# A decode step on one core: paired group semaphores, and the projection and second FFN product computed the other way round

## The chip, the cores and the metric

The kernel runs on one core of a Trainium2 chip. The metric is the device time of one execution in microseconds, taken as the median of several runs; lower is better. Beside the times there is one profiled execution, from which every duration below comes. PE is the matrix engine, PEld its weight loads, DVE the vector engine, ACT the scalar engine, POOL is GpSimd, and SP is the queue that issues the DMAs.

## The reference

It is one decode token for a batch of two. The input `x` is layer-normalised; attention with 32 heads over a cache of 8192 positions and a small dense network both read the result, and both outputs are added to `x`:

```python
# x: (2, 1, 512); caches: (2, 32, 8192, 128); wq: (512, 4096); wo: (4096, 512)
# w1: (512, 1792); w2: (1792, 512); all bf16
xn = layernorm(x)
q = (xn @ wq) split into 32 heads
p = softmax(q @ k_cache.T * 128 ** -0.5)
o = p @ v_cache
y = relu(xn @ w1) @ w2
return x + o.reshape(2, 1, 4096) @ wo + y
```

The two caches are 268 MB together. The weights add 12 MB.

## The kernel before

**Pairs.** The 64 combinations of batch and head are worked off two at a time, so there are 32 pairs. A pair's K is one tile of 4 MB (`ks`, two buffers), its V another (`vs`, two buffers). In a tile, each of the 128 partitions holds 128 cache rows of 128 elements. These 128 rows are taken in 16 groups of 8 (`NG`, `EG`).

**One step on PE** (L337 to L361) does this for a pair: for each group it transposes the 8 blocks of K into PSUM (`tp`, L301), DVE or ACT copies them to SBUF (`kT`, L416), and two groups later PE forms the scores with the query (`Sc`, L308). Which engine copies a group is set by `ON_ACT`. Between and after these, PE multiplies the previous pair's probabilities with its V (`weighted`, L321). In the middle of that it does two small matmuls for the softmax maximum (L356, L359). The steps run in a hardware loop of 16 passes with two pairs each; each engine counts the pairs in a register, which it compares with the semaphores.

**Semaphores per group.** Group `e` has its own two: `pT[e]`, raised when its transposes are done, and `kR[e]`, raised when its copy is done. They go up by one per pair, and the wait is for the pair's number `n`. SP waits for the last group's `pT` before it loads the K after next into the same buffer (L189), and for `sW` before it loads the next V (L191).

**Order of the DMAs.** Everything large goes through SP's queue in program order: `wq` (into `vs[1]`), `w1`, `w2`, then K and V of the pairs in turn, then the last V in two halves with semaphores of their own (`dH`), then `wo` in five pieces of 14, 7, 6, 3 and 2 blocks (`cuts`), each with its own semaphore (`dWo`). All five are issued some 30 us before the end, and they land in the order in which they were issued.

**Start.** Before the loop PE forms the queries (L247) and the first FFN product (L260); then the second FFN product with the activations as the stationary operand. The 2 activation columns are padded to 32 (`CT`), so that the four quarters of the 512 outputs go to four column groups of the array: 14 x 4 matmuls of 128 moving columns (L278). Four more matmuls add the input `x` (L286). The result `y` is a tile of 128 partitions, of which eight rows hold values: a quarter and a batch entry each. DVE copies it to `ys`.

**Tail.** After the loop PE sums the softmax denominators (L376), multiplies the last probabilities with the last V (L321), and rearranges the result (L386, L391) into `OX`, again padded to 32 columns. Then it multiplies with `wo` in the same manner: `OX` is stationary, and each of the 32 blocks of `wo` gives four matmuls of 128 moving columns, one for each quarter (L405), which wait piece by piece. DVE adds `ys` (L512), and SP stores the eight rows (L166). A last wait on GpSimd and the clearing of the semaphores end the program.

Of the kernel before, what the change touches and what calls it, by code (L numbers as in the profile page):

```python
# [11 lines left out]
R = 2  # L12
EG = 8
NG = 16
REP = 32
ON_ACT = (0, 3, 5, 8, 11, 13)


@with_exitstack
def kernel(  # L20
# [39 lines left out]

    CT = P // KT
    CB = CT // Bsz
    assert KT * Bsz * CB == P
    ctx.enter_context(tc.tile_critical(no_gpsimd_drain=True))
# [18 lines left out]
    kT = [sb([P, EG, P], bf16, f"kT{i}") for i in range(4)]  # L83
    identb = sb([P, P], bf16, "identb")
    sel = sb([H, DQ, P], bf16, "sel")
    onesh = sb([P, 2, P], f32, "onesh")
# [22 lines left out]
    Ob = sb([H, Bsz, Dh], bf16, "Ob")  # L109
    OX = sb([P, WJ, CT], bf16, "OX")  # L110
    hT = sb([P, FJ, CT], bf16, "hT")
    ys = sb([P, P], f32, "ys")
    osb = sb([P, P], bf16, "osb")
    onex = sb([Bsz, CT], bf16, "onex")

# [17 lines left out]
    dV = [sem(f"dV{i}") for i in range(R)]  # L133
    dH = [sem(f"dH{i}") for i in range(2)]
    dW = [sem(f"dWo{i}") for i in range(5)]
    sG, sI, sQ, sQ1 = sem("sG"), sem("sI"), sem("sQ"), sem("sQ1")
    sV, sA, sE = sem("sV"), sem("sA"), sem("sE")
    sS, sT, sB, sW = sem("sS"), sem("sT"), sem("sB"), sem("sW")
    pT = [sem(f"pT{e}") for e in range(NG)]
    kR = [sem(f"kR{e}") for e in range(NG)]  # L140
    sM, sX, sP, sO, sN = sem("sM"), sem("sX"), sem("sP"), sem("sO"), sem("sN")
# [6 lines left out]
    cuts = (0, 14, 21, 27, 30, WJ)  # L148
    NC = len(cuts) - 1
    qp = ot[0][0:QG * Bsz, :]  # L150
    tpq = tp[1][:].rearrange("p g k -> p (g k)")[:, 0:N].rearrange(
# [5 lines left out]
    hp = ot[1][:, 0:FJ * Bsz].rearrange("p (j b) -> p j b", b=Bsz)  # L157
    y = Sc[1][:, 0:P]
    fin = ot[0][:, 0:P]

    def cols(ap, c):
        return ap[c * CT:(c + 1) * CT, :]


    def store(eng):
        eng.dma_start(  # L166
            out.rearrange("b s (c p) -> c (b s) p", p=P),
            osb[0:P - CB + 1:CB, :],
        ).then_inc(dO, 16)

# [10 lines left out]
    @(lambda f: f(nc.sync))  # L181
    def _(sp):
        sp.dma_start(w1_sb, B_w1.rearrange("(p kt) f -> p kt f", kt=KT)).then_inc(dW1, 16)  # L183
        sp.dma_start(w2_sb, B_w2.rearrange("(p j) n -> p j n", j=FJ)).then_inc(dW2, 16)  # L184
        load_k(0)
        load_k(1)
        load_v(0)
        for t in range(NP - 2):
            sp.wait_ge(pT[NG - 1], t + 1)  # L189
            load_k(t + R)  # L190
            sp.wait_ge(sW, t + 1)  # L191
            load_v(t + 1)
        sp.wait_ge(sW, NP - 1)
        for i in range(2):
            sl = slice(i * SLOT // 2, (i + 1) * SLOT // 2)
            sp.dma_start(  # L196
                vs[(NP - 1) % R][:, sl], V_all[(NP - 1) * P:NP * P, sl]
            ).then_inc(dH[i], 16)
        for c in range(NC):
            sl = slice(cuts[c], cuts[c + 1])  # L200
            sp.dma_start(wo_sb[:, sl, :], wo_v[:, sl, :]).then_inc(dW[c], 16)  # L201
        sp.wait_ge(sE, 1)
        store(sp)


    @(lambda f: f(nc.gpsimd))
    def _(g):
# [16 lines left out]
        for u in range(2):  # L224
            g.memset(onesh[u * HP:(u + 1) * HP, u, :], 1.0).then_inc(sI, 1)
            g.wait_ge(sI, 3 + u)
        g.memset(OX[:], 0.0).then_inc(sI, 1)
        g.wait_ge(sV, 100)
# [8 lines left out]
    def _(pe):  # L237
# [38 lines left out]
        for j in range(FJ):  # L276
            for c in range(KT):
                pe.matmul(  # L278
                    cols(y, c),
                    lhsT=hT[:, j, :],  # L280
                    rhs=w2_sb[:, j, c * P:(c + 1) * P],
                    start=(j == 0),
                    stop=False,
                )
        for c in range(KT):
            i = pe.matmul(  # L286
                cols(y, c),
                lhsT=onex[:],
                rhs=xsb[:, c * P:(c + 1) * P],
                start=False,  # L290
                stop=True,
            )
# [5 lines left out]
        def transposes(r, e):  # L298
            for i in range(EG):
                kk = e * EG + i  # L300
                t = pe.transpose(tp[e % 4][:, i, :], ks[r][:, kk * Dh:(kk + 1) * Dh], identb[:])  # L301
            t.then_inc(pT[e], 1)

        def scores(r, e, n):
            pe.wait_ge(kR[e], n)
            for i in range(EG):
                kk = e * EG + i
                t = pe.matmul(  # L308
                    Sc[r][:, 2 * kk:2 * kk + 2 * REP],
                    lhsT=kT[e % 4][:, i, :],  # L310
                    rhs=rep(q2[r][:]),
                    start=True,
                    stop=True,
                )
            if e == NG - 1:
                t.then_inc(sS, 1)
# [19 lines left out]

        def step(r, n, n16):  # L337

# [3 lines left out]
            for e in range(NG):  # L342
                transposes(r, e)
                if e >= 2:
                    scores(r, e - 2, n)
            v = 1 - r
            values(v, n, n16)
            weighted(v, 0)
            scores(r, NG - 2, n)
            weighted(v, 1)  # L350
            scores(r, NG - 1, n)
            for e in range(2, NG):
# [9 lines left out]

        reg = nc.alloc_register(mybir.EngineType.PE, "pairno")
        pe.reg_mov(reg, 0)
        with pe.Fori(16, 16 * (NP // R) + 1, 16) as n16:
            for r in range(R):
                pe.reg_add(reg, reg, 1)
                step(r, reg, n16)

# [5 lines left out]
        for u in range(2):  # L375
            t = pe.matmul(dbp[:, :, u], lhsT=onesh[:, u, :], rhs=RS[:], start=True, stop=True)  # L376
        t.then_inc(sH, 1)
        for i in range(2):
            pe.wait_ge(dH[i], 16)
            for e in range(i * NG // 2, (i + 1) * NG // 2):  # L380
# [20 lines left out]
        for c in range(NC):  # L401
            pe.wait_ge(dW[c], 16)
            for j in range(cuts[c], cuts[c + 1]):
                for k in range(KT):
                    t = pe.matmul(  # L405
                        cols(fin, k),
                        lhsT=OX[:, j, :],
                        rhs=wo_sb[:, j, k * P:(k + 1) * P],
                        start=(j == 0),
                        stop=(j == WJ - 1),  # L410
                    )
        t.then_inc(sH, 1)

    def kcopy(eng, e):
        fn = eng.copy if e in ON_ACT else eng.tensor_copy
        fn(kT[e % 4][:], tp[e % 4][:]).then_inc(kR[e], 1)  # L416


    @(lambda f: f(nc.vector))
    def _(v):  # L420
        v.memset(eps_t[:], eps).then_inc(sV, 1)
        v.memset(onesb[:], 1.0)
        v.memset(xz[:], 0.0).then_inc(sZ, 1)
        v.memset(onex[:], 0.0)
        v.memset(hT[:], 0.0).then_inc(sZ, 1)
        v.memset(prm[R - 1][:], 0.0).then_inc(sP, 1)
# [16 lines left out]
        v.wait_ge(sQ, 1)  # L443
        v.wait_ge(sI, 1)
        v.wait_ge(sZ, 1)
# [5 lines left out]
        ).then_inc(sV, 1)  # L451
        v.wait_ge(sZ, 2)
        v.tensor_copy(onex[:, 0:CT:CB], identb[0:Bsz, 0:Bsz])
        v.wait_ge(sF, 1)
        v.tensor_scalar(
            out=hT[:, :, 0:CT:CB], in0=hp, scalar1=0.0, scalar2=None, op0=ALU.max,
        ).then_inc(sF, 1)
# [6 lines left out]
        v.wait_ge(sF, 3)  # L464
        v.tensor_copy(ys[:], y).then_inc(sF, 1)

        def pair(i, n):
            for e in range(NG):
                if e not in ON_ACT:
                    v.wait_ge(pT[e], n)  # L470
                    kcopy(v, e)
            v.wait_ge(sS, n)
# [11 lines left out]

        reg = nc.alloc_register(mybir.EngineType.DVE, "pairno_v")
        v.reg_mov(reg, 0)
        with v.Fori(0, NP // R):
            for r in range(R):
                v.reg_add(reg, reg, 1)
                pair(r, reg)  # L490

# [14 lines left out]
        v.wait_ge(sH, 3)  # L506
        v.wait_ge(sI, 5)
        v.tensor_copy(
            OX[:, :, 0:CT:CB], Sc[1][:, 0:Bsz * WJ].rearrange("p (b j) -> p j b", b=Bsz)
        ).then_inc(sV, 1)  # L510
        v.wait_ge(sH, 4)
        v.tensor_tensor(out=osb[:], in0=fin, in1=ys[:], op=ALU.add).then_inc(sE, 1)  # L512


    @(lambda f: f(nc.scalar))
    def _(a):
# [9 lines left out]

        def pair(i, n, t):
            for e in range(NG):
                if e in ON_ACT:
                    a.wait_ge(pT[e], n)  # L530
                    kcopy(a, e)
            a.wait_ge(sB, n)
# [15 lines left out]
        a.copy(nm[0][:, 0:1], eps_t[:]).then_inc(sO, 1)  # L548
        reg = nc.alloc_register(mybir.EngineType.Activation, "pairno_a")
        a.reg_mov(reg, 0)  # L550
        with a.Fori(0, NP // R) as tr:
            for r in range(R):
                a.reg_add(reg, reg, 1)
                pair(r, reg, tr * R + r)
# [28 lines left out]
```

## Time and profile before

| | us |
|---|---|
| median of 5 runs | 662.39 (662.02 to 662.48) |
| the profiled execution's own time | 662.47 |
| its span on the core | 660.5 |
| PE busy | 555.3 |
| DVE busy | 254.1 |
| ACT busy | 255.8 |

The span is the time between the first and the last instruction that the profile keeps; 2.0 us of the execution's time lie around it. A line of the groups names the source line, the engine, the operation, what it writes and reads, and the number of such instructions, then their busy time and the mean of one. A line of a timeline has the start, the length, and in brackets how long the engine stood idle before it and what released it; "issue" there means that it waited for nothing that the profile shows. The DMA row has one digit for each fortieth of the span, the mean busy share of the 16 DMA engines in tenths. Matmuls are pipelined, so that a group's length is less than its number times the time of one.

Three groups that the change touches, and one that stands for the loop:

```profile
L301 PE MATMUL tp<-identb,ks 128*128 128x128 bf16 x4096 | 324.3, 229 | 71.4 <-DMA ks<-in_A_k_cache_dram 71.4
L278 PE MATMUL Sc<-w_sb,hT 128*32 128x128 bf16 x56 | 1.7, 312 | 0.2 <-DVE hT L455 0.2
L286 PE MATMUL Sc<-xsb,onex 2*32 2x128 bf16 x4 | 0.3, 283 | 0.0
L405 PE MATMUL ot<-w_sb,OX 128*32 128x128 bf16 x128 | 3.5, 250 | 4.5 <-DMA w_sb<-in_A_wo_dram 3.5 <-DVE OX L508 0.6 <-issue 0.3
```

### The profile page before, as it was taken

To read this page: it belongs to the slowest core of one execution; us is meant where nothing else is said; L and a number is where in the kernel's file an instruction comes from. 1 tells how busy PE (TensorE), PEld (TensorE's weight loads), DVE (VectorE), ACT (ScalarE), POOL (GpSimd) and SP (SyncE) were. 2 spreads that over 40 slices of the span, in tenths; PEclk is the share of its full clock that TensorE was granted. 3 is DMA by queue.
4 is the path that set the end of the run, shared out by engine and by line. 5 is a ranking of instruction groups with operands and counts; after the bars stand their busy time and mean duration, and the time that the engine had idled before them with its cause. 6 is when DMAs were issued, how large, how long until landed. Compare 5 with 4: busy or idle time off the path is not lost.

```text
span 660.5 us, 26934 instructions
## 1 busy us (share of the span) xinstructions
PE 555.3 (84%) x12774; PEld 533.8 (81%) x12774; DVE 254.1 (38%) x438; ACT 255.8 (39%) x403; POOL 9.5 (1%) x45
## 2 busy tenths in 40 slices
PE   1788899987989878879987887997878898887894
PEld 0487898987879878879987887987878898887893
DVE  1143344442434433334443343443434344343341
ACT  1034445442434434434353433344343443433330
POOL 2000000000000000000000000000000000000000
PEclk9799999998998988999898899898989998898997
DMA  8999999999999999999999999999999999999995
GB/s 364 431 439 427 429 433 431 437 427 433 431 433 437 427 433 429 433 439 427 433 429 433 439 427 433 429 433 437 425 437 429 433 437 425 437 429 433 437 419 237
DMA packets 10539, 280.67 MB, mean 425 GB/s; under 512 B 1182, under 2 KB 1184, under 8 KB 1696
## 3 DMA queue, kind: packets, MB, share of 16 engines
q1 hardware_dynamic: 10524, 280.50, 98.9%
q8 instruction: 9, 0.15, 0.1%
q14 instruction: 2, 0.02, 0.0%
q10 hardware_dynamic: 4, 0.00, 0.0%
HBM read 280.50 MB, written 0.00 MB: 425 GB/s over the span
## 4 chain that ended last, share of the span: by engine, by line
DMA 58%; PE 37%; ACT 2%; issue 1%; SPq 1%; ACTq 0%; DVE 0%
DMA ks<-in_A_k_cache_dram 54%; PE tp L301 21%; PE Sc L308 11%; DMA w_sb<-in_A_wo_dram 5%; PE ot L321 4%; ACT kT L416 2%; ACT L416 1%; SPq L201 0%; PE Sc L356 0%; SPq L196 0%; PE Sc L359 0%; PE ot L405 0%; SPq L184 0%; SPq L183 0%; SPq L177 0%
## 5 line engine op out<-in xcount | busy, mean ns | idle before, releaser
L301 PE MATMUL tp<-identb,ks 128*128 128x128 bf16 x4096 | 324.3, 229 | 71.4 <-DMA ks<-in_A_k_cache_dram 71.4
L416 DVE COPY kT<-tp 128x1024 bf16<-128x1024 bf16 x320 | 219.7, 691 | 329.5 <-PE tp L301 329.2
L301 PEld LDWEIGHTS tp<-identb,ks 128*128 128x128 bf16 x4096 | 255.8, 103 | 75.3 <-DMA ks<-in_A_k_cache_dram 74.7
L416 ACT COPY kT<-tp 128x1024 bf16<-128x1024 bf16 x192 | 194.3, 1012 | 235.7 <-PE tp L301 235.6
L308 PE MATMUL Sc<-q,kT 128*128 128x64 bf16 x4096 | 217.1, 196 | 8.2 <-ACT kT L416 5.5
L308 PEld LDWEIGHTS Sc<-q,kT 128*128 128x128 bf16 x4096 | 178.8, 100 | 11.3 <-ACT kT L416 8.8
L321 PE MATMUL ot<-prm,vs 128*128 128x64 bf16 x4224 | 156.1, 192 | 3.2 <-issue 3.2
L321 PEld LDWEIGHTS ot<-prm,vs 128*128 128x128 bf16 x4224 | 139.1, 97 | 6.1 <-issue 3.4
L533 ACT COPY nm<-Sc 128x2 f32<-128x2 f32 x32 | 5.1, 160 | 120.9 <-PE Sc L359 120.9
L537 ACT ACTIVATE prm<-Sc,nm 64x128 bf16<-64x128 f32 x64 | 25.8, 404 | 4.3
L475 DVE TENSOR_REDUCE mcol<-Sc 64x1 bf16<-64x128 f32 x64 | 18.6, 291 | 17.6 <-PE Sc L308 17.2
L416 ACT ACT_TABLE_LOAD x16 | 20.5, 1283 | 2.2
L247 PE MATMUL ot<-vs,xz 128*16 128x512 bf16 x32 | 9.6, 474 | 8.1 <-DMA vs<-in_A_wq_dram 8.1
L480 DVE TENSOR_REDUCE mx<-Sc 1x2 bf16<-1x128 bf16 x32 | 8.9, 278 | 16.9 <-PE Sc L356 16.9
L247 PEld LDWEIGHTS ot<-vs,xz 128*16 128x16 bf16 x32 | 3.3, 106 | 14.0 <-issue 11.7
L232 POOL COPY q<-qb 128x2 bf16<-128x2 bf16 x32 | 5.8, 184 | 588.7 <-PE Sc L308 566.1
L525 ACT COPY OTf<-ot 128x2 f32 x32 | 5.1, 160 | 22.4 <-PE ot L321 22.4
L537 ACT ACTIVATION_READ_ACCUMULATOR prm<-Sc,nm x64 | 11.8, 184 | 0.0
L449 DVE TENSOR_SCALAR qs<-ot 16x512 bf16<-16x512 f32 x1 | 0.7, 680 | 17.6 <-PE ot L247 17.6
L405 PE MATMUL ot<-w_sb,OX 128*32 128x128 bf16 x128 | 3.5, 250 | 4.5 <-DMA w_sb<-in_A_wo_dram 3.5
L356 PE MATMUL Sc<-identb,mcol 128*1 128x128 bf16 x32 | 7.0, 217 | 0.0
L405 PEld LDWEIGHTS ot<-w_sb,OX 128*32 128x32 bf16 x128 | 2.2, 106 | 5.6 <-DMA w_sb<-in_A_wo_dram 4.5
(55 smaller groups left out, 36.3 us busy)
## 6 DMA issues: line engine op xcount, KB each, us to landing
ks<-in_A_k_cache_dram SPq DMA_DIRECT2D x32, 4096.0 KB, 26.7
vs<-in_A_v_cache_dram SPq DMA_DIRECT2D x31, 4096.0 KB, 31.3
vs<-in_A_wq_dram SPq DMA_DIRECT2D x1, 4096.0 KB, 12.4
vs<-in_A_v_cache_dram SPq DMA_DIRECT2D x2, 2048.0 KB, 19.3
w_sb<-in_B_w_dram SPq DMA_DIRECT2D x2, 1792.0 KB, 18.1
w_sb<-in_A_wo_dram SPq DMA_DIRECT2D x1, 1792.0 KB, 25.3
w_sb<-in_A_wo_dram SPq DMA_DIRECT2D x1, 896.0 KB, 27.0
w_sb<-in_A_wo_dram SPq DMA_DIRECT2D x1, 768.0 KB, 28.4
```

The lines of the kernel that those rows point to most:

```text
L232: g.tensor_copy(q2[t % R][:], qb[:, 2 * t:2 * t + 2]).then_inc(sQ1, 1)
L247: i = pe.matmul(qp, lhsT=xz[:, kt, Z - g * Bsz:Z - g * Bsz + QG * Bsz], rhs=vs[1][:, (kt * QG + g) * 512:(kt * QG + g + 1) * 512], start=( ...
L301: t = pe.transpose(tp[e % 4][:, i, :], ks[r][:, kk * Dh:(kk + 1) * Dh], identb[:])
L308: t = pe.matmul(Sc[r][:, 2 * kk:2 * kk + 2 * REP], lhsT=kT[e % 4][:, i, :], rhs=rep(q2[r][:]), start=True, stop=True,)
L321: t = pe.matmul(ot[r][:, 0:2 * REP], lhsT=vs[r][:, kk * Dh:(kk + 1) * Dh], rhs=rep(prm[r][:, kk, :]), start=(kk == 0), stop=(kk == KB - 1),)
L356: pe.transpose(tr_of(r), mcol[r][:], identb[:]).then_inc(sT, 1)
L405: t = pe.matmul(cols(fin, k), lhsT=OX[:, j, :], rhs=wo_sb[:, j, k * P:(k + 1) * P], start=(j == 0), stop=(j == WJ - 1),)
L416: fn(kT[e % 4][:], tp[e % 4][:]).then_inc(kR[e], 1)
L475: m = v.tensor_reduce(out=mcol[i][half, :], in_=S_of(i)[half, :, u], axis=AX.X, op=ALU.max)
L480: v.tensor_reduce(out=mx[i][:], in_=tr_of(i).rearrange("o (u m) -> o u m", u=2), axis=AX.X, op=ALU.max, negate=True,).then_inc(sX, 1)
L525: a.copy(OTf[:, bass.ds(c, 2)], ot[r][:, 0:2]).then_inc(sO, 1)
L537: x = a.activation(out=prm[i][half, :, u], in_=S_of(i)[half, :, u], func=ACTF.Exp, bias=nm[i][half, u:u + 1], scale=1.0, accum_out=RS[half ...
```

## The change

It has three parts.

**Semaphores.** Groups `e` and `e + 8` share one `pT` and one `kR`. In pair `n` the first raises it to `2n - 1` and the second to `2n`, so that each engine keeps two more registers with these values. The two halves of the last V are counted on `dW1` and `dW2`, which the FFN weights used at the start, and the first piece of `wo` on `dX`, which the load of `x` used; these waits are for 32 in place of 16. There are 19 semaphores fewer. Which engine copies which group stays the same.

**Second FFN product.** The 2 activation columns are stationary without padding, and all 512 columns of a block of `w2` move: 14 matmuls. DVE adds `x` when it takes the result out, so that `ys` is 2 x 512 in f32.

**Projection with `wo`.** Each 128 x 128 part of `wo` is the stationary operand and the 2 columns of `OX` move; the result has the outputs along the partitions, 8 columns in all. The FFN result with `x` is put in first, by four f32 matmuls with a 2 x 2 identity, ahead of the last V's product. At the end the 8 columns are copied, transposed on PE to 8 rows, copied again, and stored.

```diff
-    pT = [sem(f"pT{e}") for e in range(NG)]
-    kR = [sem(f"kR{e}") for e in range(NG)]
+    HG = NG // 2
+    pT = [sem(f"pT{e}") for e in range(HG)]
+    kR = [sem(f"kR{e}") for e in range(HG)]
...
+    last = [(dW1, 32), (dW2, 32)]
+    piece = [(dX, 32)] + [(sem(f"dWo{c}"), 16) for c in range(1, NC)]
...
-            sp.wait_ge(pT[NG - 1], t + 1)
+            sp.wait_ge(pT[HG - 1], 2 * (t + 1))
...
-        store(sp)
+        sp.dma_start(
+            out.rearrange("b s (c p) -> (b s c) p", p=P), osb[:]
+        ).then_inc(dO, 16)
+    def advance(eng, n, h):
+        eng.reg_add(n, n, 1)
+        eng.reg_add(h[0], h[1], 1)
+        eng.reg_add(h[1], h[1], 2)
...
-        g.memset(OX[:], 0.0).then_inc(sI, 1)
+        g.memset(ident2[:], 0.0).then_inc(sG, 1)
+        g.wait_ge(sG, 5)
+        g.affine_select(
+            out=ident2[:], in_=ident2[:], compare_op=ALU.not_equal, fill=1.0,
+            base=0, pattern=[[-1, Bsz]], channel_multiplier=1,
+        ).then_inc(sI, 1)
...
         for j in range(FJ):
-            for c in range(KT):
-                pe.matmul(cols(y, c), lhsT=hT[:, j, :],
-                    rhs=w2_sb[:, j, c * P:(c + 1) * P], start=(j == 0), stop=False)
-        for c in range(KT):
-            i = pe.matmul(cols(y, c), lhsT=onex[:],
-                rhs=xsb[:, c * P:(c + 1) * P], start=False, stop=True)
+            i = pe.matmul(y, lhsT=hT[:, j, :], rhs=w2_sb[:, j, :],
+                start=(j == 0), stop=(j == FJ - 1))
...
-            t.then_inc(pT[e], 1)
+            t.then_inc(pT[e % HG], 1)
-        def scores(r, e, n):
-            pe.wait_ge(kR[e], n)
+        def scores(r, e, h):
+            pe.wait_ge(kR[e % HG], h[e // HG])
...
         t.then_inc(sH, 1)
+        for k in range(KT):
+            pe.matmul(fin[:, k, :], lhsT=ys[:, k * P:(k + 1) * P], rhs=ident2[:],
+                start=(k == 0), stop=False)
         for i in range(2):
-            pe.wait_ge(dH[i], 16)
+            pe.wait_ge(*last[i])
...
-                    t = pe.matmul(cols(fin, k), lhsT=OX[:, j, :],
-                        rhs=wo_sb[:, j, k * P:(k + 1) * P],
-                        start=(j == 0), stop=(j == WJ - 1))
+                    t = pe.matmul(fin[:, k, :], lhsT=wo_sb[:, j, k * P:(k + 1) * P],
+                        rhs=OX[:, j, :], start=False,
+                        stop=(j == WJ - 1 and k == KT - 1))
         t.then_inc(sH, 1)
+        pe.wait_ge(sV, 106)
+        pe.transpose(tp[1][0:Bsz * KT, 0, :],
+            yT[:].rearrange("p b c -> p (b c)"), identb[:]).then_inc(sH, 1)
...
-        v.tensor_copy(ys[:], y).then_inc(sF, 1)
+        v.tensor_tensor(out=ys[:], in0=y, in1=xsb[:], op=ALU.add).then_inc(sF, 1)
...
         v.wait_ge(sH, 4)
-        v.tensor_tensor(out=osb[:], in0=fin, in1=ys[:], op=ALU.add).then_inc(sE, 1)
+        v.tensor_copy(yT[:], ot[0][:, 0:KT * Bsz].rearrange("p (b c) -> p b c", c=KT)).then_inc(sV, 1)
+        v.wait_ge(sH, 5)
+        v.tensor_copy(osb[:], tp[1][0:Bsz * KT, 0, :]).then_inc(sE, 1)
```

## The prediction

> **What bounds the kernel now.** I read the page first, then what the DMA queue waited for, then the last 20 us as a timeline, then that stretch in small windows.
>
> ```profile
> span 660.5 us, 26934 instructions
> DMA  8999999999999999999999999999999999999995
> q8 instruction: 9, 0.15, 0.1%
> ks<-in_A_k_cache_dram SPq DMA_DIRECT2D x32, 4096.0 KB, 26.7
> SPq L172 <- PE tp L301: 432.1, 30, 41.6
> ```
>
> The DMA row is full in all but the first and last slice: 280.5 MB bound the time. A K load lands 26.7 us after its issue, though 4 MB take 9.8 us at 430 GB/s; so some 17 us of transfers are ahead of each K load, and whatever makes SP issue a few us later in the loop costs nothing. What can move the time is the first slice, the last one, and the end. q8 carries nine instruction packets of 16 KB; they matter below.
>
> ```profile
> 643.75 4.07 PE L321 MATMUL ot<-prm,vs 128*128 128x64 bf16 x128
> 649.61 0.83 PE L405 MATMUL ot<-w_sb,OX 128*32 128x128 bf16 x45 [0.58 <-DVE OX L508]
> 650.75 0.35 PE L405 MATMUL ot<-w_sb,OX 128*32 128x128 bf16 x11 [0.31 <-issue]
> 651.70 0.57 PE L405 MATMUL ot<-w_sb,OX 128*32 128x128 bf16 x28 [0.60 <-DMA w_sb<-in_A_wo_dram]
> 656.58 0.40 PE L405 MATMUL ot<-w_sb,OX 128*32 128x128 bf16 x8 [1.55 <-DMA w_sb<-in_A_wo_dram]
> 657.04 0.29 DVE L512 TENSOR_TENSOR osb<-ot,ys 128x128 bf16<-128x128 f32 x1 [7.56 <-PE ot L405]
> 657.36 0.71 SPq L166 DMA_DIRECT2D out_dram<-osb  x1
> ```
>
> At the end PE waits for wo's pieces; the fifth (2 of 32 blocks) lands last, then come eight matmuls, one add, the store. But that landing is odd (start and length, busy time of PE, PEld, DVE, ACT, POOL, then clock, DMA share, GB/s):
>
> ```profile
> 654.40:654.70 0.30, 0.19 (x9) 0.18 (x12) 0.00 (x0) 0.00 (x0) 0.00 (x0) 0.50 0.06 21
> 654.72:655.48 0.76, 0.31 (x12) 0.04 (x4) 0.00 (x0) 0.00 (x0) 0.00 (x0) 0.50 0.00 0
> 655.48:655.74 0.26, 0.00 (x0) 0.00 (x0) 0.00 (x0) 0.00 (x0) 0.00 (x0) 0.50 0.06 8
> ```
>
> wo is through by 654.70 but for one 2 KB row, which moves alone at 655.49. By the trace's packet records an instruction packet of 16,384 B starts at 654.396 and takes 1.11 us; the row follows at its end, so both sit on one DMA engine. By the semaphore records 15 of the fifth piece's 16 increments are in by 655.107, the last at 656.536. **The end of the kernel hangs on one instruction fetch: 1.43 us.**
>
> Where does it come from? PE stops for instructions ("issue") at times. In the loop's first pass it stops after 62 weighted matmuls of pair 0 (stall ending at 50.33), in the tail after 45 wo matmuls (650.74). Counted in the code, 636 load-matmul pairs and 9 waits, register and branch steps lie between, 1281 instructions: 5 times 256 and one. So a block is 256 instructions, and each boundary that PE passes asks for the block after the next. From a stall's end to the next packet it took 4.67 us (50.33 to 55.00), 3.63 (57.47 to 61.10), 4.75 (69.76 to 74.51) and 3.66 (650.74 to 654.40). That last packet lies beyond the program's end: useless, yet it holds wo.
>
> [...]
>
> **The change part by part.**
>
> *Shared semaphores.* Pair n raises a shared counter from 2n-2 to 2n-1 (group e) and 2n (group e+8), so every wait opens on the same event as before; SP's wait on the last group too. Two more register steps per pair on PE, DVE and ACT (32 to 42 ns each in the trace's records) hide in PE's 71.4 us of waiting for K and the engines' longer ones; without that cover they would be 32 x 2 x 0.04 = 2.6 us. At the end 72 semaphores (66 named in the code, 6 of the frame) are cleared one by one from 659.76 to 660.13, 5.2 ns each; 19 fewer: -0.10 us. The late loads' semaphores are only other counters: 0.
>
> *FFN2 at the start.* 60 column-tiled matmuls (26.90 to 28.81) become 14 of 512 columns. L247 has that shape: 9.61 us for 32, 0.30 each, at most 0.43: 4.2 to 6.0 us, so done by 31.1 to 33.0. K of pair 0 lands at 32.98 (PE idles 4.18 us before it): hidden. If it ran over, K2's issue at 45.45 would slip; the 20.4 MB queued ahead last until about 49.5, 4 us of cover. DVE's add waits in front of the first copy at 34.91: also covered. GpSimd swaps the OX memset (0.96 us) for two small operations, 20 us before its next job.
>
> *Residual as four f32 matmuls in the tail.* L376 shows two f32 matmuls as four load-matmul pairs, 0.109 us apart; four make eight: 0.87 us. 128 weighted matmuls, OX and wo queue behind: wo's start moves from 649.61 to 650.48. That is cover as long as wo's pieces land later than PE gets to them.
>
> *wo with weights stationary.* 128 full loads of 128 columns with 2 moving. The nearest rows: L321, contiguous weights, load 97 ns, 4.07 us for 128, 31 ns each; and L260, 2 moving columns but weights at a stride, load 163 ns, 3.52 us for 56, 60 ns. The wo slice is contiguous, so I take 31. Pieces one and two are done at 652.2 and 653.1, piece three lands about 653.5 and ends at 654.3, four (654.47) at 654.9: PE waits for the fifth.
>
> [...]
>
> *The code moves.* Before wo stand 46 pairs fewer (FFN2: -92 instructions), one register move, some 2 register steps and eight pairs more (+19): -73. Boundaries stay, so that after 45 wo matmuls falls after 81, and the one before it, now after weighted matmul 51 (645.3), after 88 (644.62 + 2.73 = 647.4). Its block took 5.4 us to be there (650.74): now 652.8, when PE reaches matmul 81 at 653.0; up to 0.5 us of stall would be lost in PE's waits. Past it the useless packet is asked for at 652.8 or later; with 3.6 to 4.75 us it starts after 656.4, and wo is through at 654.7. **So the fifth piece lands at about 655.11: -1.43 us.**
>
> *The tail.* From landing to store, now 656.54 to 657.36: 0.82. After: wake 0.04, eight matmuls 7 x 0.031 + 0.20 = 0.42, hop 0.03, copy of 128x8 0.165 (L446), hop 0.05, transpose 0.224 (L386), hop 0.04, copy of 8x128 0.22 (between L453's 0.149 and L505's 0.280), hop 0.03: 1.22, +0.40. Bounds: 1.05, and 1.6 at half clock with both copies at 0.28. PE waits on the first copy and DVE on the transpose, with only the store behind them. The store has 8 plain rows in place of a 4x2 pattern: its issue takes 0.71, SP's others 0.33 to 0.43, the small x load 0.55 (ACT's queue). I take the slowest of SP's own, 0.43: -0.28 (0 to -0.38).
>
> **Sum:** -1.43 + 0.40 - 0.28 - 0.10 = -1.41. The profiled run took 662.47 (span 660.5, 2.0 around it), the median 662.39: 661.06 and 660.98; I say **661.0**.
>
> **Rivals.**
> 1. *The packet still meets wo's last row.* Delays of under 2 us would do it. For: nothing fixes the delay, and queues are thinner at the end. Against: all four measured are 3.6 or more. The 1.43 is then not gained: 662.39 + 0.40 - 0.38 = 662.4.
> 2. *PE starves at matmul 81.* If the block takes 7.2 us (4.75 + 2.45 from packet to release) it arrives at 654.6; 47 matmuls are left, 1.5 us, 0.65 later than forecast: 661.7, at worst 662.3.
> 3. *Slower: the weight load at 60 ns.* Should 2 moving columns, not the stride, be what makes L260 slow, PE becomes the bound: 650.48 + 128 x 0.06 + 0.17 = 658.33; then 0.76 to the store, 659.1 against 657.36, less 0.38: +1.36, 663.75. It decides from 38 ns on and is a loss from 49. The load's own 163 against 97 ns speaks against it.
> 4. *Other groups released too early or late by the shared counts:* excluded by the order of increments, and the DMA cover would hide some us.
>
> **How the numbers follow.** Forecast 0.66 (660.5 to 661.5), first rival 0.14, second 0.10, third 0.08, the rest 0.02. The range 660.4 to 662.8 takes in the first three. 0.2% is 1.32 us, about what a measurement here tells from no change: faster means below 661.07, slower above 663.71. The forecast lies on the first edge, its sum just past it; I put two thirds of it below, as most terms could still come out cheaper: faster 0.45. Its other third and rivals one and two make the same 0.45; slower 0.10.
>
> **What would show it.** The fifth piece's matmuls begin near 655.15, with no DMA in a lone late window; the "issue" gap in wo goes from matmul 45 to about 81; eight f32 pairs of about 0.9 us before the weighted run; wo spaced by about 31 ns; from the last wo matmul to the store two copies and a transpose, 0.76 us. I am wrong if the last row still moves alone, if wo's load takes 163 ns, or if a slice of the loop loses DMA share.

## The result, and the profile after

The changed kernel takes 660.69 us in the median (660.50 to 661.47 over 25 runs); beside it the kernel before took 662.27 (660.87 to 662.57 over 45 runs). The ratio, which is taken over the means, is 0.9979, with a 95% interval of 0.9974 to 0.9985: 1.4 us less, and 1.58 between the medians. The profiled execution took 660.65 us against 662.47.

First the page of the changed kernel, with its DMA row and its instruction queue:

```profile
span 658.6 us, 26862 instructions
...
DMA  8999999999999999999999999999999999999996
...
q8 instruction: 9, 0.15, 0.1%
```

The loop runs as before: the slices between the first and the last are full as they were, and there are nine instruction packets as before. The last slice has a 6 where it had a 5. The span is 1.9 us shorter, so look at the end. The timeline of the changed kernel from 640 us on (start, length, what, idle time before it and its releaser):

```profile
642.40 1.05 PE L379 MATMUL ot<-ident,ys 2*128 2x2 f32 x8
643.38 4.08 PE L322 MATMUL ot<-prm,vs 128*128 128x64 bf16 x128
...
649.34 1.54 PE L413 MATMUL ot<-OX,w_sb 128*128 128x2 bf16 x56 [0.69 <-DMA w_sb<-in_A_wo_dram]
651.44 0.91 PE L413 MATMUL ot<-OX,w_sb 128*128 128x2 bf16 x28 [0.56 <-DMA w_sb<-in_A_wo_dram]
653.35 1.39 PE L413 MATMUL ot<-OX,w_sb 128*128 128x2 bf16 x36 [1.01 <-DMA w_sb<-in_A_wo_dram]
654.98 0.38 PE L413 MATMUL ot<-OX,w_sb 128*128 128x2 bf16 x8 [0.24 <-DMA w_sb<-in_A_wo_dram]
655.39 0.17 DVE L517 CAST yT<-ot 128x8 bf16<-128x8 f32 x1 [6.47 <-PE ot L413]
655.61 0.27 PE L422 MATMUL tp<-identb,yT 128*8 128x128 bf16 x1 [0.26 <-DVE yT L517]
655.92 0.21 DVE L519 COPY osb<-tp 8x128 bf16<-8x128 bf16 x1 [0.36 <-PE tp L422]
656.16 0.37 SPq L195 DMA_DIRECT2D out_dram<-osb  x1
```

The last eight matmuls start at 654.98, not at 656.58: PE waits 0.24 us for the fifth piece, where it waited 1.55. Behind them stand the two copies and the transpose; still the store is issued at 656.16 in place of 657.36. The small windows of the changed kernel (start and length, busy time of PE, PEld, DVE, ACT, POOL, then clock, DMA share, GB/s):

```profile
654.10:654.40 0.30, 0.20 (x8) 0.14 (x6) 0.00 (x0) 0.00 (x0) 0.00 (x0) 0.50 0.51 157
654.42:655.48 1.06, 0.70 (x20) 0.53 (x17) 0.09 (x1) 0.00 (x0) 0.00 (x0) 0.50 0.00 0
655.48:656.50 1.02, 0.27 (x1) 0.08 (x1) 0.29 (x2) 0.00 (x0) 0.00 (x0) 0.50 0.00 0
```

No row of data moves after 654.40; the lone late row is gone. By the packet records the ninth instruction packet still comes, at 654.376 for 1.10 us, but no row of wo starts after it; the last one started at 654.312. The fifth piece's last increment comes at 654.931, 1.605 us earlier than before (656.536).

The difference of the two profiled executions adds up: landing -1.61; from the landing to the issue of the store 1.23 in place of 0.82, +0.41; from that issue to the store's last increment 1.195 in place of 1.727, -0.53; the clearing of the semaphores 330 ns in place of 421, -0.09. The sum is -1.82, and the times differ by 1.82.

### The profile page after: what moved, and what is told of

It is laid out like the page before. It is cut to its first block, busy times and chain, and to the rows that moved or that the text cites. A ratio compares the mean times of both kernels' runs of the same rounds, so it can differ in the third digit from the quotient of the medians.

```text
span 658.6 us, 26862 instructions
## 1 busy us (share of the span) xinstructions
PE 558.0 (85%) x12737; PEld 534.6 (81%) x12737; DVE 253.2 (38%) x436; ACT 255.9 (39%) x403; POOL 9.2 (1%) x46
## 4 chain that ended last, share of the span: by engine, by line
DMA 58%; PE 36%; ACT 2%; issue 2%; SPq 1%; ACTq 0%; DVE 0%
DMA ks<-in_A_k_cache_dram 54%; PE tp L302 21%; PE Sc L309 11%; PE ot L322 4%; DMA w_sb<-in_A_wo_dram 4%; ACT kT L431 2%; ACT L431 1%; SPq L193 0%; PE Sc L357 0%; SPq L188 0%; PE Sc L360 0%; SPq L176 0%; SPq L175 0%; SPq L169 0%; PE ot L413 0%
## 5 line engine op out<-in xcount | busy, mean ns | idle before, releaser
L413 PE MATMUL ot<-OX,w_sb 128*128 128x2 bf16 x128 | 4.1, 166 | 2.6 <-DMA w_sb<-in_A_wo_dram 2.5
L413 PEld LDWEIGHTS ot<-OX,w_sb 128*128 128x128 bf16 x128 | 3.7, 101 | 3.0 <-DMA w_sb<-in_A_wo_dram 2.2
```

Source lines behind the costliest of these rows:

```text
L413: t = pe.matmul(fin[:, k, :], lhsT=wo_sb[:, j, k * P:(k + 1) * P], rhs=OX[:, j, :], start=False, stop=(j == WJ - 1 and k == KT - 1),)
```

## The experiments

The theory: what the change gained is the instruction packet that no longer holds back wo's last row, and whether it does so is a matter of when PE passes the code boundary in the tail. The rivals: the smaller semaphore count, the new form of the products, or the cheaper store made the gain.

**Less code alone.** The kernel before, with the loop of the second FFN product over 5 of the 14 blocks of `w2`. The other nine blocks are left out of the sum, and with them 72 PE instructions:

```diff
-        for j in range(FJ):
+        for j in range(5):
```

> The kernel before, with the second FFN product summed over 5 of its 14 blocks (nine blocks of w2 are left out). PE's program is 72 instructions shorter ahead of wo; semaphores, wo and the tail are as before. Packet theory: the last instruction packet moves behind wo, the fifth piece lands near 655.1, and the time falls by 1.3 to 1.5 us, to about 660.9. Rivals: if fewer semaphores or the new form of wo and its tail made the gain, this stays within 0.2 us of the kernel before, 662.3.

Measured: 660.96 us, ratio 0.9986 (0.9977 to 0.9995). The timeline of this kernel:

```profile
653.59 1.92 PE L405 MATMUL ot<-w_sb,OX 128*32 128x128 bf16 x44 [0.96 <-DMA w_sb<-in_A_wo_dram]
...
655.56 0.29 DVE L512 TENSOR_TENSOR osb<-ot,ys 128x128 bf16<-128x128 f32 x1 [6.59 <-PE ot L405]
655.88 0.71 SPq L166 DMA_DIRECT2D out_dram<-osb  x1
```

The matmuls of the fourth and fifth piece run as one group without a pause; the packet starts at 654.472 and the last increment is at 655.060. The old form of the products, with the old semaphores and the old store, gains nearly all of it. So none of the rivals is needed.

**The old code position in the changed kernel.** 36 small matmuls into an unused part of PSUM, early in the program, put the boundary back to where it was in the code:

```diff
         i.then_inc(sQ, 1)
+        for _ in range(36):
+            pe.matmul(ot[1][:, 256:258], lhsT=identb[:], rhs=identb[:, 0:2],
+                start=True, stop=True)
         pe.wait_ge(sV, 6)
```

> The changed kernel with 36 more load-matmul pairs on PE at the start, into PSUM columns that nobody reads, while PE waits for wq. They put the 72 instructions back. Packet theory: the block boundary falls after about 46 wo matmuls again, a row of wo waits behind the packet, and 1.2 to 1.5 us are lost: about 662.0. Rivals (semaphores, form of wo): 660.7, as the changed kernel.

Measured: 660.80 us, ratio 0.9981 (0.9972 to 0.9990). A miss: the gain stayed. The windows and then the timeline of this kernel show why:

```profile
643.50:646.00 2.50, 2.50 (x60) 2.48 (x61) 0.00 (x0) 0.00 (x0) 0.00 (x0) 0.69 1.00 424
```

```profile
650.59 2.35 PE L415 MATMUL ot<-OX,w_sb 128*128 128x2 bf16 x84 [0.32 <-DVE OX L515]
653.47 1.43 PE L415 MATMUL ot<-OX,w_sb 128*128 128x2 bf16 x36 [0.52 <-DMA w_sb<-in_A_wo_dram]
```

In the weighted products the granted clock was 0.69 (1.00 in the changed kernel's profile), 60 matmuls in 2.5 us instead of 86. PE came to wo at 650.59 rather than 649.34 and passed the boundary that much later in time. The packet started at 654.298, earlier than in the kernel before, and still all rows of its engine were ahead of it (six rows start later, on other engines, as this one is taken until 655.399): last increment 655.002. So the place in the code alone is not what decides; when PE gets there is. Whether the runs without a profile had that clock too is not shown; ten of the eleven runs lie between 660.68 and 660.92, one at 662.27.

**The boundary further forward.** The same with 72 in place of 36 matmuls.

> The changed kernel with 72 unused load-matmul pairs on PE at the start, twice those of the run before. Now the block boundary falls after about 10 wo matmuls, so that PE passes it near 649.5, over a microsecond earlier than with 36. Request theory (what counts is when PE passes the boundary, some 3 us before the packet starts): the packet starts at 652.4 to 653.1, rows of wo wait behind it, and the time is 661.8 to 662.1. Rival (the changed kernel's wo form or tail is immune to the packet): 660.7 to 660.9.

Measured: 662.08 us, ratio 0.9999 (0.9990 to 1.0008). The whole gain is gone, with the change otherwise complete. Windows of this kernel:

```profile
654.68:655.33 0.65, 0.32 (x12) 0.23 (x9) 0.00 (x0) 0.00 (x0) 0.00 (x0) 0.50 0.00 0
655.33:656.00 0.67, 0.00 (x0) 0.00 (x0) 0.00 (x0) 0.00 (x0) 0.00 (x0) 0.50 0.07 9
```

After a gap of 0.65 us with no data, a few rows move alone: by the records three of 2 KB, behind a packet that started at 654.245. The last increment is at 656.455. This is the picture of the kernel before. The time is as expected, but the packet's start is not: 652.4 to 653.1 was expected. PE came to wo only at 650.71, as the granted clock was 0.68 in the weighted products here too.

**Shared semaphores alone.** The kernel before with part one of the change only.

```diff
-    pT = [sem(f"pT{e}") for e in range(NG)]
-    kR = [sem(f"kR{e}") for e in range(NG)]
+    pT = [sem(f"pT{e}") for e in range(HG)]
+    kR = [sem(f"kR{e}") for e in range(HG)]
...
+    last = [(dW1, 32), (dW2, 32)]
+    piece = [(dX, 32)] + [(sem(f"dWo{c}"), 16) for c in range(1, NC)]
...
```

> The kernel before with the shared semaphores alone (19 fewer; one PE instruction more). Packet theory: 0.09 us less for the clearing, 662.2, and the last row still alone behind the packet. Semaphore theory: most of the 1.6 us, about 660.7. Form-of-wo theory: 662.3.

Measured: 662.27 us, ratio 0.9995 (0.9986 to 1.0004). Windows of this kernel:

```profile
654.42:655.02 0.60, 0.38 (x12) 0.11 (x5) 0.00 (x0) 0.00 (x0) 0.00 (x0) 0.50 0.00 0
655.02:656.00 0.98, 0.00 (x0) 0.00 (x0) 0.00 (x0) 0.00 (x0) 0.00 (x0) 0.50 0.06 13
```

and its timeline at the boundary:

```profile
650.33 0.35 PE L418 MATMUL ot<-w_sb,OX 128*32 128x128 bf16 x12 [0.16 <-issue]
```

PE passes the boundary 0.4 us earlier than before (a stall ending at 650.33 against 650.75), the packet starts 0.46 us earlier, at 653.938, and six rows are behind it in place of one. The first three take 0.23 us each and the others 0.08 to 0.13; the last is through at 655.97, and the last increment is at 656.386.

**The other way round: own semaphores in the changed kernel**, 19 more, parts two and three kept.

```diff
-    pT = [sem(f"pT{e}") for e in range(HG)]
-    kR = [sem(f"kR{e}") for e in range(HG)]
+    pT = [sem(f"pT{e}") for e in range(NG)]
+    kR = [sem(f"kR{e}") for e in range(NG)]
...
```

> The changed kernel with a semaphore of its own for each group and each late load (19 more; one PE instruction fewer). Packet theory: 0.09 us more than the changed kernel, 660.8. Semaphore theory: 662.2. Form-of-wo theory: 660.7.

Measured: 660.95 us, ratio 0.9982 (0.9973 to 0.9991), 0.26 us above the changed kernel's 660.69; in the profiles wo's last increment is 0.18 us later (655.11) and the clearing of the semaphores 0.09 longer. In this profile the granted clock was 0.69 in the weighted products, PE came to wo only at 651.60, and the packet started at 655.032, when all of wo had been moved. The two tests put the shared semaphores' worth between nothing and 0.26 us; an interval of these ratios reaches 0.6 us to either side.

**A longer wait, and nothing else.** The kernel before, with PE held back until the second piece of wo is in:

```diff
         pe.wait_ge(sV, 105)
+        pe.wait_ge(dW[0], 16)
+        pe.wait_ge(dW[1], 16)
```

> The kernel before, with one edit: PE waits for wo's second piece as well (landed at 651.65) before it starts on the first. Nothing is removed or moved; PE starts on wo 2 us later. Request theory: the boundary after 45 wo matmuls is passed near 651.9 in place of 650.7, the packet starts at about 654.5 or later, and the longer wait gains 1.2 to 1.5 us: 660.8 to 661.1. Code-size theory (only the shorter program helps): 662.3. If the late start itself cost something, over 662.3.

Measured: 661.01 us, ratio 0.9983 (0.9974 to 0.9992). The timeline of this kernel:

```profile
651.78 3.67 PE L407 MATMUL ot<-w_sb,OX 128*32 128x128 bf16 x128 [2.74 <-DMA w_sb<-in_A_wo_dram]
655.50 0.29 DVE L514 TENSOR_TENSOR osb<-ot,ys 128x128 bf16<-128x128 f32 x1 [5.99 <-PE ot L407]
655.81 0.71 SPq L166 DMA_DIRECT2D out_dram<-osb  x1
```

PE idles 2.74 us where it idled 0.58 and the kernel is 1.2 us faster. No code was moved by more than two instructions. The packet starts at 654.415, at the time when it started before (654.396), but it was asked for after 651.78, and all rows of its engine are ahead of it (one row starts later, on another engine, at 654.476): last increment 654.998. Of all runs this one shows most directly that the packet made the old end late.

**The gate, the shared semaphores and a split store.** If the old tail is shorter and only its store dear, the two together should beat the changed kernel; the store is split into two of four rows, on SP's and ACT's queue.

```diff
+        pe.wait_ge(*piece[0])
+        pe.wait_ge(*piece[1])
...
-        store(sp)
+        store(sp, 0)
...
+        a.wait_ge(sE, 1)
+        store(a, 1)
```

> The kernel before with the shared semaphores, the same wait for wo's second piece, and the store as two DMAs of 4 plain rows, one on SP's queue and one on ACT's. It keeps the short tail (one add). Against the changed kernel: tail 0.4 us shorter, store equal or up to 0.2 dearer: 660.2 to 660.6. If the two stores do not shorten the landing, 660.8.

Measured: 661.08 us, ratio 0.9984 (0.9975 to 0.9993). A miss: not faster than the gate alone (661.01), and 0.39 us above the changed kernel by the medians. The timeline of this kernel:

```profile
655.82 0.67 SPq L169 DMA_DIRECT2D out_dram<-osb  x1
655.82 0.60 ACTq L169 DMA_DIRECT2D out_dram<-osb  x1
```

Four rows cost 0.60 to 0.67 us to issue, nearly as much as the eight rows in the 4x2 pattern (0.71), while the changed kernel's eight plain rows cost 0.37. From the issue to the last increment it took 1.93 us, against 1.195. So the old short tail with a dear store and the new long tail with a cheap one come out close: from wo's last increment to the end of the execution it takes 6.00 us in the gated kernel's profile (661.00 - 655.00) and 5.72 in the changed kernel's (660.65 - 654.93), and 0.09 of the difference is the clearing of the semaphores. No version here has a lower median than the changed kernel.

**Too much code.** 91 small matmuls in the kernel before shift the boundaries until there are ten packets.

```diff
+        for _ in range(91):
+            pe.matmul(ot[1][:, 256:258], lhsT=identb[:], rhs=identb[:, 0:2],
+                start=True, stop=True)
```

> The kernel before with 91 unused load-matmul pairs on PE at the start: the program is 182 instructions longer, its boundaries in the tail lie nearly where the changed kernel has them (after 82 wo matmuls), and there are ten packets, the ninth at about 649 in place of 654.4. If the ninth goes to the engine that the first one had delayed already, as the lone late row in the kernel before suggests, wo lands near 656.2 and the time stays at 662.0 to 662.3. If packets go round all 16 engines, 660.9.

Measured: 662.37 us, ratio 1.0006 (0.9997 to 1.0015), a little above the 662.0 to 662.3 expected if the ninth packet goes to an engine that is late already. The timeline of this kernel:

```profile
652.90 0.94 PE L407 MATMUL ot<-w_sb,OX 128*32 128x128 bf16 x28 [1.93 <-DMA w_sb<-in_A_wo_dram]
654.75 1.99 PE L407 MATMUL ot<-w_sb,OX 128*32 128x128 bf16 x44 [0.91 <-DMA w_sb<-in_A_wo_dram]
```

The ninth packet comes at 649.77, in the middle of wo, and one engine is late in every piece from then on: the third piece's last increment is at 654.709, the one before it at 653.841; the fifth piece's last is at 656.298. Here the packet that came while wo was on its way delayed its engine's rows to the end of the stream.

## Why the prediction was right, and where it was off

It said 661.0 us; 660.69 were measured, -1.41 forecast against -1.58 between the medians. The main term held: the end hung on one instruction packet, and the change moved that out of the way. The table has the kernels in the order in which PE asks for the last packet. That time is an estimate from the starts and stalls in the timelines, good to some 0.3 us, as PE's sequencer runs ahead of the array (in the kernel before it is at a wait behind the loop at 642.469, while the loop's last matmul starts at 642.737); for the kernel with own semaphores it is worked out from the block's packet at 650.891 and the 2.49 us given below. The kernel with ten packets is left out, and so is the split store, which has the gate's landing (655.00):

| kernel | asked for | packet starts | wo's last increment | median us |
|---|---|---|---|---|
| shared semaphores | 650.3 | 653.938 | 656.386 | 662.27 |
| before | 650.7 | 654.396 | 656.536 | 662.27 |
| changed, 72 more | 650.7 | 654.245 | 656.455 | 662.08 |
| changed, 36 more | 651.4 to 652 | 654.298 | 655.002 | 660.80 |
| changed | 651.5 | 654.376 | 654.931 | 660.69 |
| less code | 651.75 | 654.472 | 655.060 | 660.96 |
| before, gated | after 651.78 | 654.415 | 654.998 | 661.01 |
| changed, own semaphores | about 653.4 | 655.032 | 655.11 | 660.95 |

Now the steps one by one.

- **"starts after 656.4" was wrong by 2 us.** The packet started at 654.376; wo's last row started only 0.06 us ahead of it, where the forecast had room for 1.7. Two things failed. The block was there at about 651.5, not at 652.8: its own packet started at 649.027, and from there to the release it takes 2.49 us (648.254 to 650.74 in the kernel before; there the four stalls of the loop's first pass that end from 50.33 to 69.76 lie 256 PE instruction records apart, and each ends 2.46 to 2.56 us after a packet's start). PE was early: the last weighted products began at 643.38 and not at 644.62, and wo at 649.34 and not at 650.48. PE came to L376 at 641.87, in the kernel before at 643.31; the granted clock from 620 to 630 us was 1.00 here and 0.83 there, which is the likely reason. And the delay from the request to the packet was about 2.9 us, less than the four delays of 3.6 to 4.75 that the step rested on. With own semaphores, where the packet met no rows, it was about 1.6. So these runs show no fixed delay to reckon with: 1.6 to 4.75 us.
- **What divides the cases is the packet's place among the rows of its engine.** The packet records show this place. On one engine a row of 2 KB starts 80 ns after the one before it, and an engine's share of a load ends with a packet of 4 bytes (1172 of them in the kernel before: 16 for each of 73 loads, and 4 for the store). In the changed kernel, with 36 more, with less code and in both gated kernels the instruction packet starts 5 or 6 ns after such a 4-byte packet: 654.370 and 654.376 in the changed kernel. Its engine had nothing of wo left. In the kernel before, with the shared semaphores and with 72 more it starts 80 ns after a row (654.316 and 654.396 in the kernel before), where the next row would stand, and that row comes 1.09 or 1.10 us later. The table has the same division by the request: up to 650.7 us rows fall behind the packet, from about 651.4 on none. So the packet's start by itself is no measure: 654.245 is too early, 654.298 is not, and 654.396 is again too early. That the packet comes behind those rows which stand ahead of it on its engine when the request is made is the author's reading, which fits both; no run shows the request itself, nor how many rows that are. The order of issue does not set the place: all of wo was issued by 626.5, long before any of these requests.
- **The landing came out in part by luck.** By the step's own reckoning a start at 654.376 is the first rival. What saved the term is that PE asked some 0.8 us later than in the kernel before, and not the 2 us that were forecast.
- **"-73 instructions" was only one way to get there.** The step named the code position as the cause. Less code alone does it, but PE arriving later does it as well, by a slower clock (36 more matmuls) or a longer wait (the gate).
- **The landing**, -1.43 forecast, was -1.61: the packet's 1.43 is there. The other 0.18 is that all 16 increments were in by 654.931, where the first 15 of the kernel before were in at 655.107; for this no step had a reason.
- **The "issue" gap at matmul 81** did not come: the gaps are after 56, 84 and 120 matmuls, each at a wait for a piece. The second rival falls with it.
- **The tail** was right: 1.23 us from the landing to the store, 1.22 forecast.
- **The store** was mis-sized: -0.53 in place of -0.28. The issue itself went from 713 to 372 ns (-0.34, forecast -0.28); the first packet then left 0.79 us after the issue began, in place of 1.31, so that the way from the issue to the last increment was 0.19 us shorter on top. The "slowest of SP's own", 0.43, was misread: the first two K loads take 0.53 and 0.48 us to issue.
- **The semaphores**: the clearing went from 421 to 330 ns, -0.09 for -0.10 forecast. In the end time it can't be told from nothing.
- **The second FFN product** was hidden, as forecast; timeline of the changed kernel at the start:

```profile
25.81 4.87 PE L287 MATMUL Sc<-w_sb,hT 128*2 128x512 bf16 x14
...
30.71 0.68 DVE L475 TENSOR_TENSOR ys<-Sc,xsb 2x512 f32<-2x512 f32 x1 [4.45 <-PE Sc L287]
32.91 1.32 PE L302 MATMUL tp<-identb,ks 128*128 128x128 bf16 x16 [2.24 <-DMA ks<-in_A_k_cache_dram]
```

  4.87 us, within the 4.2 to 6.0 given, and PE then still waits 2.24 us for K.
- **The f32 residual** took 1.05 us for 0.87 forecast; hidden, as PE waited for wo four times afterwards.
- **The third rival**, a weight load and its matmul at 60 ns, did not come. The groups of the changed kernel after 640 us:

```profile
L413 PE MATMUL ot<-OX,w_sb 128*128 128x2 bf16 x128 | 4.1, 166 | 2.6 <-DMA w_sb<-in_A_wo_dram 2.5
L413 PEld LDWEIGHTS ot<-OX,w_sb 128*128 128x128 bf16 x128 | 3.7, 101 | 3.0 <-DMA w_sb<-in_A_wo_dram 2.2 <-DVE OX L513 0.8
```

  The load takes 101 ns, as L321's contiguous weights did (97), not L260's 163; 128 pairs take 4.1 us, 32 ns each.

Five of the 45 runs of the kernel before lie between 660.87 and 661.25, where the kernels with a free last row lie, and the other 40 between 661.6 and 662.57. In the two series of experiments three and four of its 33 runs lie as low (660.92 to 661.18), and so do two of 11 with the shared semaphores (660.78 and 661.14). The other way round, one run of 11 with less code took 662.82, and one with 36 more 662.27. It may be that PE came to the boundary later or earlier in those runs, and the packet with it; no profile caught one.

## What to carry to other kernels

Where a kernel ends on a stream of loads, look at which transfer lands last, and whether it comes late on one DMA engine alone: what holds it may be no data at all, here 16 KB of PE code that by the prediction's count lies beyond the program's end. Here the delay depended on the time at which PE passed a point of its code, so that an edit ahead of it, even an idle wait, could gain or lose 1.2 to 1.6 us; test an edit's own worth with this held the same. And do not judge a store's issue by its size: here eight plain rows were issued in 0.37 us, four in 0.60 to 0.67.

## What the runs showed of the hardware

- The instruction packets of 16 KB took 1.02 to 1.11 us each in the profiles of the two kernels, and the last one of the kernel before made a single increment of the fifth piece late: 15 were in by 655.107, the last at 656.536. In the tail half of the increments come late: of the fourth piece's in the kernel before, eight come between 652.26 and 652.93 and eight between 653.93 and 654.47. Eight packets had gone by then; after seven packets seven were late (of the V load that landed at 625.664, nine increments come between 623.444 and 624.127 and seven from 625.339 on). With ten packets one increment of wo's third piece is late again beyond the others (654.709 after 653.841). To which engine a packet goes was not shown.
- How long SP or ACT took to issue a DMA did not go by its size: 0.33 to 0.53 us for the loads of 128 partitions, 0.37 for the store of eight plain rows, 0.55 for the two rows of `x`, 0.60 to 0.67 for four rows, 0.71 for a pattern of 4x2. Of the store's 16 increments, four come with its rows in the kernel before, whose pattern is 4x2, and eight in the changed kernel, whose eight rows are plain; the other increments come in one step, 0.58 and 0.65 us ahead of the first of these.
